# Two transformer layers on one core: where a layernorm's tiles are transposed, and what sums the attention heads

## The chip, the core and the metric

The kernel runs on one core of one Trainium2 chip. The metric is the device time of one launch in microseconds (us). Lower is better. The engines are named as in the profile: PE (TensorE, the matrix engine), DVE (VectorE), ACT (ScalarE), POOL (GpSimd) and SP (SyncE, which here only issues DMAs).

## The reference

Two layers over a sequence of 2048 tokens of 1024 features, with the same weights in both layers. Each layer is a sliding, dilated local attention and a dense block, each with a layernorm in front and a residual addition behind:

```python
x = x + attn(layernorm(x))     # wqkv: 1024 x 3072, wo: 1024 x 1024
x = x + dense(layernorm(x))    # w1: 1024 x 3584, gelu (tanh), w2: 3584 x 1024, b1, b2

# attn: 32 heads of 32 features; each token s sees 8 keys, at s, s-2, ..., s-14
logits[h, s, w] = sum_d q[h, s, d] * k[h, s - 2 * w, d] * scale      # masked where s - 2 * w < 0
p = softmax(logits, over w)
o[h, s, d] = sum_w p[h, s, w] * v[h, s - 2 * w, d]
```

## The kernel before

**Groups and stages.** A group is 512 tokens of one layer, so there are N = 8 groups, n = 0 to 7 (four for each layer). For each group PE runs four stages: qkv(n) (`gen_qkv`), WO(n) (`gen_wo`), FFN1(n) (`gen_ffn1`) and FFN2(n) (`gen_ffn2`). Their order on PE is written out by hand at the end of the kernel: qkv(0), qkv(1), the first 18 of 24 chunks of qkv(2), WO(0), the last 6 chunks of qkv(2) (they belong to V), FFN1(0), FFN2(0); then for n = 1 to 5: WO(n), qkv(n+2), FFN1(n), FFN2(n); then WO(6), WO(7), FFN1(6), FFN2(6), FFN1(7), FFN2(7). A chunk is one accumulator: 8 matmuls of 128x128 by 128x512 into one of six PSUM tiles `acc`, which ACT (qkv, FFN1) or DVE (WO, FFN2) empties.

**Order on the engines.** The stages are generators that yield after each chunk. `stage(gen, count, sides)` runs one and calls side functions after given chunks: `at(u, f, ...)` calls f after chunk u, `each(f, n, u0, du, c0, c1)` calls f(n, c) at regular chunks. PE's instructions keep the order in which the program issues them. ACT, DVE, POOL and SP are wrapped in `InOrder`, which can hold the same: `hold()` makes everything that DVE is given later come after what it was given before; between holds the scheduler orders DVE by itself. Every engine then works through its list in order, and an instruction that waits holds up all that stand behind it on that engine. `dep_order(a, b, why)` puts a behind b in the order of their engine without a wait.

**Layernorm and transposes.** Before qkv (`ln_a`) and after WO (inside `gen_wo`), `ln_tile` takes a tile of 128 tokens, computes its statistics (DVE), the inverse deviation `rstd` (POOL) and the normalized tile `xn` (DVE), and brings it into `xnT`, with the features on the partitions, as PE needs it. Usually that is one `dma_start_transpose` on SP's queue for each tile of 128x1024. In WO(0) only tiles 0 and 1 go this way; tiles 2 and 3 are put on the list `late`, and `transpose_late` transposes them on PE (`transpose_on_pe`: 8 matmuls with `ident` into an `acc`, then a copy by ACT), after chunk 4 of the last six chunks of qkv(2).

**Weights.** All weights stream through `wpool` (tile `wt`, five buffers of 1 MB) by DMAs on SP's queue, which also carries the transposes. FFN1 loads W1 in seven pieces, one for each four chunks (`j4`).

**Attention.** DVE multiplies q with eight shifted views of k, one product for each of eight feature slices c (`new_prod(n, c)`, tile `big`, three buffers), and adds the eight products in a tree. What is left holds, on 128 partitions, four feature parts of each of 32 heads, and these four must be summed. For groups 0 and 1 PE does it in `head_sum`: 8 matmuls of 128x32 by 128x512 with the 0/1 matrix `smat`, into the PSUM tile `L`. For groups 2 to 7 `gather(n)` issues four DMAs of 256 KB on POOL's queue which copy the product (SBUF to SBUF, `big<-big`) so that the four parts lie side by side, and `attend(n)` adds them by three DVE additions into `e`. `attend` then does the softmax (maximum and subtraction on DVE, Exp on ACT, sum, reciprocal and multiplication on DVE); `spread` copies the weights to all parts of a head through DRAM; `av(n, c)` multiplies them with eight shifted views of v and adds up the output `oT`. The sides of FFN1(n) hold attend(n+2) and most of av(n+1), those of qkv(n+2) the first av(n+1) and, by `gen_qkv`, the products of group n+2.

Of the kernel before, what the change touches and what calls it, by code (L numbers as in the profile page):

```python
# [17 lines left out]
def kernel(  # L18
# [188 lines left out]
    def transpose_on_pe(xn, out, pst=None, halves=1):  # L207
        if pst is None:
            pst = psum.tile([P, KD, P], BF16, name="acc", bufs=6)
        for k in range(KD):  # L210
            pe(nc.tensor.transpose(pst[:, k, :], xn[:, k * P:(k + 1) * P], ident[:]))
        n = KD // halves
        for h in range(halves):
            act.copy(out[:, h * n:(h + 1) * n, :], pst[:, h * n:(h + 1) * n, :])

    late = []

    def transpose_late():
        while late:
            transpose_on_pe(*late.pop(0))  # L220

    def ln_tile(t, tt, xnT, on_pe=False, ahead=False):
        mv, rstd = (mv_ahead[:, tt, :], rstd_ahead[:, tt, :]) if ahead else ln_stats(t)
        xn = ln_norm(t, mv, rstd)
        if on_pe:
            late.append((xn, xnT[:, tt, :, :]))
            return
        sp.dma_start_transpose(xnT[:, tt, :, :], xn[:].rearrange("s (k p) -> s k p", p=P))

    first_late = []  # L230

# [32 lines left out]
        assert len(a) == 2 and a[1][0] == 1 and a[1][1] == HALO + T  # L264
        return bass.AP(tensor=t_ap.tensor, offset=t_ap.offset, ap=[list(a[0]), [DIL, W], [1, T]])

    def win_by_tile(t_ap):
        a = t_ap.ap
        assert len(a) == 2 and a[1][0] == 1 and a[1][1] == HALO + T
        return bass.AP(tensor=t_ap.tensor, offset=t_ap.offset, ap=[list(a[0]), [P, NTT], [DIL, W], [1, P]])  # L270

    st = {n: {} for n in range(N)}
    xa = {}
    xb = {}
# [9 lines left out]
    def head_sum(n, last=True):  # L284

        if "L" not in st[n]:
            st[n]["L"] = psum.tile([P, W, P], F32, name="L", bufs=1)
            start = True
        else:
            start = False  # L290
        L = st[n]["L"]
        prod = st[n]["prods"].pop(0)
        for wh in range(2):
            for tb in range(NTT):
                mm(L[tb * H:(tb + 1) * H, wh * 4:(wh + 1) * 4, :], lhsT=smat[:],
                   rhs=prod[:, tb, wh * 4:(wh + 1) * 4, :], start=start,
                   stop=last, skip_group_check=True, tile_position=(0, tb * H))

    def new_prod(n, c):

        s = st[n]
        prod = bigp.tile([P, NTT, W, P], BF16, name="big")
        q = s["qT"][:, c, :].rearrange("p (b t) -> p b t", t=P)
        vec.tensor_tensor(out=prod[:], in0=q.unsqueeze(2).to_broadcast([P, NTT, W, P]), in1=win_by_tile(s["kT"][:, c, :]), op=ALU.mult)
        tree = s["prods"]
        tree.append(prod)
        if c % 2 == 1:
            for _ in range(1 if c % (NCH // s["parts"]) == 1 else 2):
                b = tree.pop()
                vec.tensor_tensor(out=tree[-1][:], in0=tree[-1][:], in1=b[:], op=ALU.add)  # L310
# [48 lines left out]
        if g + 1 < NG:  # L359
            act.copy(vhalo[:], vT[:, :, T:T + HALO])  # L360

    def gather(n):

        s = st[n]
        prod = s["prods"].pop(0)
        Lq = bigp.tile([P, HP, W, P], BF16, name="big")
        s["Lq"] = Lq
        for tb in range(NTT):
            pool.dma_start(Lq[tb * H:(tb + 1) * H, :, :, :], prod[:, tb, :, :])

    def attend(n):

        s = st[n]
        e = smp.tile([P, W, P], F32, name="e")
        if "Lq" in s:
            Lq = s.pop("Lq")
            vec.tensor_tensor(out=e[:], in0=Lq[:, 0, :, :], in1=Lq[:, 1, :, :], op=ALU.add)
            for j in range(2, HP):
                vec.tensor_tensor(out=e[:], in0=e[:], in1=Lq[:, j, :, :], op=ALU.add)
            L = e  # L380
        else:
            head_sum(n)
            L = s.pop("L")
        if n % NG == 0:
            vec.tensor_tensor(out=L[0:H, 0:W - 1, 0:HALO], in0=L[0:H, 0:W - 1, 0:HALO], in1=mask[:], op=ALU.add)
        mx = smp.tile([P, P], F32, name="mx")
        vec.tensor_reduce(out=mx[:], in_=L[:].rearrange("p w t -> p t w"), axis=AX.X, op=ALU.max)
        vec.tensor_tensor(out=e[:], in0=L[:], in1=mx[:].unsqueeze(1).to_broadcast([P, W, P]), op=ALU.subtract)
        act.activation(e[:], e[:], ACT.Exp, scale=SCALE)
        z = smp.tile([P, P], F32, name="z")  # L390
        vec.tensor_reduce(out=z[:], in_=e[:].rearrange("p w t -> p t w"), axis=AX.X, op=ALU.add)
        vec.reciprocal(z[:], z[:])
        a = smp.tile([P, W, P], BF16, name="a")
        vec.tensor_tensor(out=a[:], in0=e[:], in1=z[:].unsqueeze(1).to_broadcast([P, W, P]), op=ALU.mult)
        s["a"] = a
# [19 lines left out]
        vec.tensor_tensor(out=pv[:, 0:2, :], in0=pv[:, 0:2, :], in1=pv[:, 2:4, :], op=ALU.add)  # L415
        vec.tensor_tensor(out=s["oT"][:, c, :], in0=pv[:, 0, :], in1=pv[:, 1, :], op=ALU.add)

    def gen_wo(n, pe_from=NTT):
        g = n % NG
        oT = st[n]["oT"]  # L420
        wts = []
        for h in range(2):
            wt = wpool.tile([P, NCH // 2, D], BF16, name="wt")
            sp.dma_start(wt[:], wo_v[:, h * (NCH // 2):(h + 1) * (NCH // 2), :])
            wts.append(wt)
        xnT = new_xnT()
        xb[n] = xnT
        for tt in range(NTT):
            t = g * NTT + tt
            for dh in range(2):  # L430
                ps = acc_tile()
                for c in range(NCH):
                    mm(ps[:], lhsT=oT[:, c, tt * P:(tt + 1) * P], rhs=wts[c // 4][:, c % 4, dh * HALF:(dh + 1) * HALF],
                       start=(c == 0), stop=(c == NCH - 1))
                xs = x[t][:, dh * HALF:(dh + 1) * HALF]
                vec.tensor_tensor(out=xs, in0=ps[:], in1=xs, op=ALU.add)
                yield
            ln_tile(t, tt, xnT, tt >= pe_from)
        del st[n]

    def gen_ffn1(n):
        xnT = xb.pop(n)
        hT = hpool.tile([P, KF, T], BF16, name="hT")
        st[("h", n)] = hT
        for j4 in range(KF // 4):
            wt = wpool.tile([P, KD, 4 * P], BF16, name="wt")
            sp.dma_start(wt[:], w1_v[:, :, j4 * 4 * P:(j4 + 1) * 4 * P])
            for jj in range(4):
                j = j4 * 4 + jj
                ps = acc_tile()  # L450
                for k in range(KD):
                    mm(ps[:], lhsT=wt[:, k, jj * P:(jj + 1) * P], rhs=xnT[:, :, k, :], start=(k == 0), stop=(k == KD - 1))
                act.activation(hT[:, j, :], ps[:], ACT.Gelu_apprx_tanh, bias=b1T[:, j:j + 1])
                yield
# [63 lines left out]
    def stage(gen, count=None, sides=()):  # L518


        u = 0
        while count is None or u < count:
            if next(gen, gen) is gen:
                break
            for v, f in sides:
                if v == u:
                    f()
            u += 1
        for v, f in sides:
            if v >= u:  # L530
                f()
# [13 lines left out]
    with tc.tile_pool(name="early", bufs=1) as early:  # L545
        load_x(1)
        load_x(2)
        stage(gen_qkv(0, qk_next=early), sides=at(14, load_b2))
        q1 = gen_qkv(1, defer=True, qk_pool=early)
        stage(q1, sides=at(6, attend, 0) + at(6, spread, 0) + at(6, hold) + each(new_prod, 1, 8, 1, 0, 4) + each(av, 0, 12, 1))  # L550
        q2 = gen_qkv(2, defer=True)
        stage(q2, 18)
        stage(gen_wo(0, 2))
        stage(q2, sides=each(new_prod, 1, 0, 1, 4, 8) + at(4, transpose_late))
    hpool = ctx.enter_context(tc.tile_pool(name="hpool", bufs=1))
    stage(gen_ffn1(0), sides=at(4, attend, 1) + at(4, spread, 1) + at(4, hold) + each(new_prod, 2, 2, 1, 0, 4) + each(av, 1, 6, 2))
    stage(gen_ffn2(0), sides=at(0, ln_stats_ahead, 3) + at(15, hold) + each(new_prod, 2, 15, 1, 4, 8) + at(23, hold) + at(23, gather, 2) + at(23, ln_a, 3, None, True))
    for n in range(1, N - 2):
        stage(gen_wo(n), sides=at(0, spread, n + 1) if n > 1 else at(7, attend, 2))
        stage(gen_qkv(n + 2), sides=(at(0, spread, 2) if n == 1 else []) + each(av, n + 1, 0, 2, 0, 3))  # L560
        gather(n + 2)
        stage(gen_ffn1(n), sides=at(20 if n == 1 else 9, attend, n + 2) + each(av, n + 1, 8, 2, 3, 8))
        if n + 3 < N:
            stage(gen_ffn2(n), sides=at(2, ln_a, n + 3))
        else:
            stage(gen_ffn2(n), sides=at(0, spread, n + 2) + each(av, n + 2, 1, 4))
# [36 lines left out]
```

## Time and profile before

| | us |
|---|---|
| median of 8 runs | 1242.12 |
| lowest and highest run | 1241.39 and 1243.43 |
| the profiled execution's own time | 1243.43 |
| its span in the profile | 1241.7 |
| PE busy in the span | 1228.4 (99%) |
| DVE, ACT, POOL busy | 864.8, 306.1, 126.6 |

The mean clock that PE was granted is 0.999. In the timeline a line reads: start, duration, engine, line of the code, operation, output<-input, shapes, count; in brackets the idle time ahead of it and what ended it. Line L93 is the helper through which all of DVE's, ACT's, POOL's and SP's instructions go, and L118 the one for PE's matmuls, so that groups are told apart by their tiles. SPq is SP's sequencer, on which the DMAs are issued.

### The profile page before, as it was taken

Reading aid. Unit: us, or ns where it says so; the run is one execution under the profiler, and the core shown is the slowest. Engines: PE = TensorE matmul, PEld = TensorE weight load, DVE = VectorE, ACT = ScalarE, POOL = GpSimd, SP = SyncE. Lnnn points to the kernel's source line nnn. Section 1 sums busy time; section 2 is a strip of 40 time slices with the busy share of each in tenths; the row PEclk is TensorE's granted clock in tenths of the full one; section 3 lists DMA queues with packets and bytes.
Section 4 is the critical chain, followed back from the end, with each engine's and each line's share of the span. In section 5 each row is a group of like instructions: output and inputs, shape, how many; then the busy total and the mean of one; then the engine's idle time right before and its main releaser. Section 6 shows DMA issues by size and latency. Waiting matters only on the chain.

```text
span 1241.7 us, 13984 instructions
## 1 busy us (share of the span) xinstructions
PE 1228.4 (99%) x5793; PEld 632.6 (51%) x5793; DVE 864.8 (70%) x886; ACT 306.1 (25%) x477; POOL 126.6 (10%) x238
## 2 busy tenths in 40 slices
PE   9999999989999999999999999999999999999998
PEld 6666544446444564445644456444554444444444
DVE  7999899985994999457995469954599598012001
ACT  3333251013430133301342013410234101310310
POOL 4010210011031102200022000210000102000000
PEclk9999999999999999999999999999999999999999
DMA  9954564595577648655577465866646667546441
GB/s 300 285 178 149 167 203 155 168 200 178 180 185 223 167 157 218 195 169 153 170 209 208 165 172 167 206 196 192 195 159 167 195 199 193 168 156 195 148 138 53
DMA packets 217247, 226.10 MB, mean 182 GB/s; under 512 B 66450, under 2 KB 185376, under 8 KB 214112
## 3 DMA queue, kind: packets, MB, share of 16 engines
q1 hardware_dynamic: 212592, 208.16, 55.0%
q0 software_dynamic: 4592, 17.05, 6.1%
q8 instruction: 45, 0.74, 0.3%
q14 instruction: 18, 0.15, 0.0%
HBM read 197.40 MB, written 6.29 MB: 164 GB/s over the span
## 4 chain that ended last, share of the span: by engine, by line
PE 59%; DVE 6%; issue 0%; ACT 0%; POOL 0%; DVEq 0%
PE acc L118 59%; DVE big L93 4%; DVE stats L93 0%; DVE e L93 0%; POOL rstd L93 0%; DVE oT L93 0%; DVE mx L93 0%; ACT L93 0%; DVE xn L93 0%; ACT e L93 0%; ACT hT L93 0%; DVE x L93 0%; DVE mv L93 0%; DVEq L93 0%
## 5 line engine op out<-in xcount | busy, mean ns | idle before, releaser
L118 PE MATMUL acc<-xnT,wt 128*128 128x512 bf16 (+1 forms) x3376 | 722.2, 376 | 7.2 <-DMA xnT<-xn 4.9
L118 PEld LDWEIGHTS <-wt 128*128 128x128 bf16 x3376 | 399.2, 119 | 328.0 <-issue 10.3
L118 PE MATMUL acc<-wt,hT 128*128 128x512 bf16 (+1 forms) x1820 | 388.1, 376 | 0.0
L118 PEld LDWEIGHTS <-hT 128*128 128x128 bf16 x1820 | 178.1, 98 | 209.0
L93 DVE TENSOR_TENSOR big<-big 128x2048 bf16<-128x2048 bf16 (+2 forms) x184 | 246.4, 1361 | 2.6
L93 ACT ACTIVATE hT<-acc,b1T 128x512 bf16<-128x512 f32 x224 | 151.6, 690 | 310.3 <-PE acc L118 309.9
L93 DVE TENSOR_TENSOR big<-abc,vT 128x4096 bf16<-128x4096 bf16 x64 | 145.1, 2289 | 68.5 <-DMA abc<-a_d 67.9
L93 DVE TENSOR_TENSOR big<-qT,kT 128x4096 bf16<-128x4096 bf16 x64 | 143.8, 2287 | 26.7 <-ACT kT L93 26.1
L93 DVE TENSOR_TENSOR tmp<-acc,b2bc 128x512 f32<-128x512 f32 x56 | 38.7, 690 | 146.4 <-PE acc L118 143.4
L93 ACT CAST qT<-acc 128x512 bf16<-128x512 f32 x64 | 37.5, 587 | 320.8 <-PE acc L118 320.7
L118 PE MATMUL acc<-wt,oT 128*128 128x512 bf16 x448 | 97.8, 379 | 0.0
L93 DVE BATCH_NORM_STATS2 stats<-x 128x6 f32<-128x512 bf16 x128 | 83.0, 679 | 4.1 <-DMA x<-in_A_x_dram 3.7
L93 POOL TENSOR_TENSOR rstd<-mv,eps_t 128x1 f32<-128x1 f32 x60 | 27.5, 459 | 451.0 <-DVE mv L93 450.9
L118 PEld LDWEIGHTS <-oT 128*128 128x128 bf16 x448 | 43.8, 98 | 52.8
L93 DVE TENSOR_TENSOR x<-acc,big 128x512 bf16<-128x512 f32 (+1 forms) x9 | 5.7, 633 | 90.0 <-PE acc L118 90.0
L93 ACT CAST vT<-acc 128x512 bf16<-128x512 f32 x64 | 37.6, 587 | 83.6 <-PE acc L118 83.6
L93 ACT CAST kT<-acc 128x512 bf16<-128x512 f32 x64 | 37.6, 587 | 71.6 <-PE acc L118 71.6
L93 DVE TENSOR_TENSOR x<-acc,x 128x512 bf16<-128x512 f32 x64 | 42.9, 673 | 5.2 <-PE acc L118 5.0
L93 POOL DMA_DIRECT2D big<-big x24 | 13.7, 578 | 296.0 <-DVE big L93 237.1
L93 POOL TENSOR_TENSOR rstd<-rstd,mhalf 128x1 f32<-128x1 f32 x60 | 43.3, 722 | 4.7
L93 DVE TENSOR_SCALAR xn<-x,mv,rstd 128x1024 bf16<-128x1024 bf16 x52 | 28.1, 543 | 18.6 <-POOL rstd L93 17.0
L93 DVE TENSOR_TENSOR x<-tmp,x 128x512 bf16<-128x512 f32 x56 | 38.7, 691 | 1.3
(60 smaller groups left out, 251.9 us busy)
## 6 DMA issues: line engine op xcount, KB each, us to landing
wt<-in_B_w_dram SPq DMA_DIRECT2D x56, 1024.0 KB, 5.7
wt<-in_B_w_dram SPq DMA_DIRECT2D x64, 896.0 KB, 4.9
wt<-in_A_wqkv_dram SPq DMA_DIRECT2D x46, 1024.0 KB, 5.6
wt<-in_A_wo_dram SPq DMA_DIRECT2D x16, 1024.0 KB, 4.9
abc<-a_d POOLq DMA_DIRECT2D x32, 256.0 KB, 5.0
big<-big POOLq DMA_DIRECT2D x24, 256.0 KB, 7.5
x<-in_A_x_dram SPq DMA_DIRECT2D x16, 256.0 KB, 6.1
out_dram<-x SPq DMA_DIRECT2D x31, 128.0 KB, 2.7
```

Source lines behind the costliest of these rows:

```text
L93: inst = f(*args, **kwargs)
L118: return pe(nc.tensor.matmul(*args, **kwargs))
```

## The change

In WO(0) all four tiles are transposed by `dma_start_transpose`; `late`, `transpose_late` and the argument `pe_from` go. The second W1 load of FFN1(0) is put behind the last of these transposes in SP's order. One product of group 1 is issued ahead of WO(0) and three after it instead of four after it, with a `hold()` on each side of WO(0), so that DVE does only WO(0)'s additions and layernorm in between. `gather` and the three additions of `attend` go: for all groups `attend` calls `head_sum` on PE. The products change their layout from [tile of 128 tokens, w, token] to [w, token], and `head_sum` reads them accordingly.

```diff
-    late = []
-
-    def transpose_late():
-        while late:
-            transpose_on_pe(*late.pop(0))
-
-    def ln_tile(t, tt, xnT, on_pe=False, ahead=False):
+    last_transpose = [None]
+
+    def ln_tile(t, tt, xnT, ahead=False):
         mv, rstd = (mv_ahead[:, tt, :], rstd_ahead[:, tt, :]) if ahead else ln_stats(t)
         xn = ln_norm(t, mv, rstd)
-        if on_pe:
-            late.append((xn, xnT[:, tt, :, :]))
-            return
-        sp.dma_start_transpose(xnT[:, tt, :, :], xn[:].rearrange("s (k p) -> s k p", p=P))
+        last_transpose[0] = sp.dma_start_transpose(xnT[:, tt, :, :], xn[:].rearrange("s (k p) -> s k p", p=P))
...
                 mm(L[tb * H:(tb + 1) * H, wh * 4:(wh + 1) * 4, :], lhsT=smat[:],
-                   rhs=prod[:, tb, wh * 4:(wh + 1) * 4, :], start=start,
+                   rhs=prod[:, wh * 4:(wh + 1) * 4, tb * P:(tb + 1) * P], start=start,
                    stop=last, skip_group_check=True, tile_position=(0, tb * H))
...
-        prod = bigp.tile([P, NTT, W, P], BF16, name="big")
-        q = s["qT"][:, c, :].rearrange("p (b t) -> p b t", t=P)
-        vec.tensor_tensor(out=prod[:], in0=q.unsqueeze(2).to_broadcast([P, NTT, W, P]), in1=win_by_tile(s["kT"][:, c, :]), op=ALU.mult)
+        prod = bigp.tile([P, W, T], BF16, name="big")
+        vec.tensor_tensor(out=prod[:], in0=s["qT"][:, c, :].unsqueeze(1).to_broadcast([P, W, T]), in1=win(s["kT"][:, c, :]), op=ALU.mult)
...
-    def gather(n):
-
-        s = st[n]
-        prod = s["prods"].pop(0)
-        Lq = bigp.tile([P, HP, W, P], BF16, name="big")
-        s["Lq"] = Lq
-        for tb in range(NTT):
-            pool.dma_start(Lq[tb * H:(tb + 1) * H, :, :, :], prod[:, tb, :, :])
-
     def attend(n):
 
         s = st[n]
-        e = smp.tile([P, W, P], F32, name="e")
-        if "Lq" in s:
-            Lq = s.pop("Lq")
-            vec.tensor_tensor(out=e[:], in0=Lq[:, 0, :, :], in1=Lq[:, 1, :, :], op=ALU.add)
-            for j in range(2, HP):
-                vec.tensor_tensor(out=e[:], in0=e[:], in1=Lq[:, j, :, :], op=ALU.add)
-            L = e
-        else:
-            head_sum(n)
-            L = s.pop("L")
+        head_sum(n)
+        L = s.pop("L")
...
+        e = smp.tile([P, W, P], F32, name="e")
...
-            ln_tile(t, tt, xnT, tt >= pe_from)
+            ln_tile(t, tt, xnT)
...
-            sp.dma_start(wt[:], w1_v[:, :, j4 * 4 * P:(j4 + 1) * 4 * P])
+            load = sp.dma_start(wt[:], w1_v[:, :, j4 * 4 * P:(j4 + 1) * 4 * P])
+            if n == 0 and j4 == 1:
+                dep_order(load, last_transpose[0], "transposes first")
...
         stage(q2, 18)
-        stage(gen_wo(0, 2))
-        stage(q2, sides=each(new_prod, 1, 0, 1, 4, 8) + at(4, transpose_late))
+        new_prod(1, 4)
+        hold()
+        stage(gen_wo(0))
+        hold()
+        stage(q2, sides=each(new_prod, 1, 0, 1, 5, 8))
...
-    stage(gen_ffn2(0), sides=at(0, ln_stats_ahead, 3) + at(15, hold) + each(new_prod, 2, 15, 1, 4, 8) + at(23, hold) + at(23, gather, 2) + at(23, ln_a, 3, None, True))
+    stage(gen_ffn2(0), sides=at(0, ln_stats_ahead, 3) + at(15, hold) + each(new_prod, 2, 15, 1, 4, 8) + at(23, hold) + at(23, ln_a, 3, None, True))
...
-        gather(n + 2)
```

The calls of attend in the sides stand where they stood: attend(2) after chunk 7 of WO(1), attend(3) after chunk 20 of FFN1(1), attend(4) to attend(7) after chunk 9 of FFN1(2) to FFN1(5), with `head_sum` at those places in PE's order.

More of the change, by code (lines that the diff above doesn't have):

```diff
@@ L265, in win @@
         return bass.AP(tensor=t_ap.tensor, offset=t_ap.offset, ap=[list(a[0]), [DIL, W], [1, T]])
[L267 to L270, printed above, removed]
     st = {n: {} for n in range(N)}
@@ L416, in av, with gen_wo @@
         vec.tensor_tensor(out=s["oT"][:, c, :], in0=pv[:, 0, :], in1=pv[:, 1, :], op=ALU.add)
-    def gen_wo(n, pe_from=NTT):
+    def gen_wo(n):
         g = n % NG
```

## The prediction

> **What bounds the kernel now.** I read the busy table first, then TensorE's (PE's) waits, then the timeline around each wait, then one-microsecond windows.
>
> ```profile
> PE 1228.4 (99%) x5793; PEld 632.6 (51%) x5793; DVE 864.8 (70%) x886; ACT 306.1 (25%) x477; POOL 126.6 (10%) x238
> ```
>
> PE is busy 99% of 1241.7 us. Work taken off VectorE (DVE, 70%) or GpSimd (POOL) is worth nothing by itself; only PE's own work and PE's pauses count. The pauses, by what ended them:
>
> ```profile
> PE acc L118 <- DMA xnT<-xn: 4.9, 1, 4.9
> PE acc L118 <- ACT hT L93: 1.8, 1, 1.8
> PE acc L118 <- DVE big L93: 1.1, 1, 1.1
> PE acc L211 <- DVE xn L93: 1.0, 1, 1.0
> ```
>
> Columns are total, count, longest. The first: qkv(3) waits for its transposed input. The second: PE waits for ScalarE (ACT) in FFN1(2). The fourth stands at WO(0)'s PE transposes. The unit of PE's time is the matmul chunk: ACT's casts follow each other every 1.726 us, 8 matmuls of 0.2158.
>
> **Part 1: WO(0)'s tiles 2 and 3 leave PE.** Around the 16 PE transposes:
>
> ```profile
> 148.27 0.59 ACT L93 CAST vT<-acc 128x512 bf16<-128x512 f32 x1 [1.14 <-PE acc L118]
> 149.69 0.62 PE L211 MATMUL acc<-ident,xn 128*128 128x128 bf16 x8 [1.00 <-DVE xn L93]
> 152.08 0.59 ACT L93 CAST vT<-acc 128x512 bf16<-128x512 f32 x1 [0.72 <-PE acc L118]
> ```
>
> Two casts lie 3.81 us apart instead of 1.73: **-2.08 us** of PE (two groups of 8 transposes, 0.61 and 0.62, and the wait of 1.00). In their place two more DMA transposes stand on SyncE (SP), and the second W1 load behind the last. WO(0) ends on PE at 139.4; 48 matmuls of V follow (10.36), so FFN1(0) needs the tiles at 149.8. With DVE held to WO(0)'s adds and layernorm, the last xn is ready near 142.55; a DMA transpose lands in 2.7 (the shortest of the transposes' rows) to 4.4 us (their median): 145.3 to 147.0, margin 2.8 to 4.5. The moved W1 load is issued near 143.9 instead of 140.65 and lands 5.7 later (its row), at 149.6; FFN1(0) needs it at 149.8 + 4 x 1.726 = 156.7. Behind it on SP wait only later W1 loads. Cost of the move: nothing, hidden by the 10.36 us of V.
>
> [...]
>
> **The delayed DVE work.** new_prod(1,5) to (1,7) now come after WO(0)'s layernorm. Seven DVE operations (15.85 us by their rows: 2.25 for one product, 4.54 for two additions, 4.52 for two products, 4.54 for two additions) follow 142.55 and end at 158.4. PE demands head_sum(1) five chunks into FFN1(0), at 149.8 + 8.63 = 158.43. With a signal's passage **+0.2 us** (0 to 1).
>
> **Part 2: the gathers go.** The largest pause is in the timeline at qkv(3):
>
> ```profile
> 249.22 13.98 PE L118 MATMUL acc<-wt,oT 128*128 128x512 bf16 x64
> 254.18 13.98 SPq L93 DMA_TRANSPOSE xnT<-xn  x3
> 268.07 17.23 PE L118 MATMUL acc<-xnT,wt 128*128 128x512 bf16 x73 [4.87 <-DMA xnT<-xn]
> 271.30 0.59 ACT L93 CAST qT<-acc 128x512 bf16<-128x512 f32 x1 [29.34 <-PE acc L118]
> ...
> 407.51 13.98 PE L118 MATMUL acc<-wt,oT 128*128 128x512 bf16 x64
> 423.25 0.59 ACT L93 CAST qT<-acc 128x512 bf16<-128x512 f32 x1 [41.33 <-PE acc L118]
> ```
>
> From the start of WO(1) to the first qT cast of qkv(3) 22.08 us pass; the same stretch at WO(2), without a pause, takes 15.74. The pause costs **6.34 us**: 4.87 of wait, the rest PE at half clock after it. Why are the transposes late? gather(2) is issued by POOL at 246.9 to 249.4, just ahead of the transposes of ln_a(3) and WO(1). Windows (PE, PEld, DVE, ACT, POOL busy; PE clock; DMA share; GB/s):
>
> ```profile
> 137.00:138.00 1.00, 1.00 (x7) 0.46 (x5) 1.00 (x4) 0.00 (x0) 0.13 (x1) 1.00 0.68 151
> 253.00:254.00 1.00, 1.00 (x7) 0.42 (x5) 1.00 (x3) 0.00 (x0) 0.00 (x0) 1.00 1.49 138
> 256.00:257.00 1.00, 1.00 (x7) 0.41 (x6) 1.00 (x3) 0.00 (x0) 0.00 (x0) 1.00 1.02 100
> 265.00:266.00 1.00, 0.00 (x0) 0.00 (x0) 1.00 (x3) 0.00 (x0) 0.00 (x0) 1.00 1.03 401
> 268.00:269.00 1.00, 0.93 (x3) 0.47 (x4) 0.94 (x2) 0.00 (x0) 0.00 (x0) 0.50 1.27 285
> ```
>
> A lone transpose (137) moves 151 GB/s at a share of 0.68. At 253 to 257 a higher share moves only 100 to 138 GB/s, while weights alone (265) reach 401: the queues are clogged, and the slowest transpose lands after 15.6 us (median 4.4). Without the gather I expect ordinary landings. FFN2(0) now ends near 247.2; the fourth xn of ln_a(3) is issued about 6 us later and lands 3 to 5 us after that (256.2 to 258.5); PE needs it at 247.2 + 13.8 + one head sum, 261.7: margin 3 to 5. So **-6.34 us**. No later gather falls on transposes that PE waits for.
>
> **Part 3: the head sums come onto PE**, once each for groups 2 to 7. Groups 0 and 1 do it already:
>
> ```profile
> 64.59 0.62 PE L118 MATMUL L<-big,smat 128*32 128x512 bf16 x8
> 64.69 0.59 ACT L93 CAST qT<-acc 128x512 bf16<-128x512 f32 x1 [1.14 <-PE acc L118]
> 67.12 0.59 ACT L93 CAST qT<-acc 128x512 bf16<-128x512 f32 x1 [1.84 <-PE acc L118]
> ```
>
> The casts are 2.43 apart, 0.70 over 1.73; at group 1 (160.71 to 163.09) 0.65. 6 x 0.68 = **+4.08 us**, all on PE's path (bounds 3.9 and 4.2). The products' layout changes to suit; products of av, which read in that order already, take 2289 ns against 2287. [...]
>
> Each head sum must find its products added up. At group 3 they are ready at 330.8, PE asks at 339.3. For the others the products start when kT is cast; at qkv(5) the tree ends at 625.65, 9.0 us after FFN1(3) starts (616.65), and PE asks 17.3 us after it: margin 8.3.
>
> **Part 4: ACT's pause in FFN1(2).**
>
> ```profile
> 504.78 1.06 ACT L93 ACTIVATE e<-e 128x1024 f32<-128x1024 f32 x1
> 507.89 5.34 PE L118 MATMUL acc<-xnT,wt 128*128 128x512 bf16 x24 [1.80 <-ACT hT L93]
> ```
>
> The Exp, and a halo copy before it, stand in ACT's order ahead of gelus; they wait for DVE, six accumulators fill, PE stops 1.80 us. Three additions of 1.22 per group go, and the maximum reads PSUM in 1.22 instead of 1.91 (group 0's row). In the changed order DVE runs, after the tree (9.0 us into FFN1): two av (8.55), two multiplies (4.41), maximum (1.2), an addition (1.14), the subtraction (1.2): 25.5. Exp follows at 25.6; it must start by 28.65 for gelu 12 to free its accumulator before chunk 18. Margin 3.1 us (3.9 in FFN1(2)); the halo copy has 3.7. So **-1.80 us**.
>
> Off the path: DVE loses 18 x 1.22 + 6 x 0.69 = 26 us, POOL 24 issues (13.7 us), the DMA queues 6.3 MB; PE was waiting for none of it elsewhere.
>
> **Sum**: -2.08 + 0.2 - 6.34 + 4.08 - 1.80 = -5.94. The profiled execution took 1243.43 (span 1241.7 and 1.73 around it), so 1237.5 on its basis; the median of the eight runs is 1242.12, so **1236.2**.
>
> **Rivals.** *The gather is not to blame*: the transposes queue behind weight loads, the 6.34 stays, and the sum is -2.08 + 0.2 + 4.08 - 1.80 = +0.4: 1242.5. For it: WO(1)'s weights are in flight at the same time. Against: transposes beside weight loads elsewhere (366 to 378, 568 to 581, 1026 to 1056) cost PE nothing. If half stays: 1239.4.
>
> *Exp blocks ACT in every FFN1(2) to (5)* (the slower side): it stands in front of gelu 12, and PE stops once Exp starts later than 28.65 us into the stage. If DVE is 5.3 us later than worked, each of four stages loses 2.2, 8.8 in all: 1245.0. For it: before has one such stop. Against: 3.1 us of margin, and DVE has idle stretches of 7.06 us ahead of the products to absorb layernorm work:
>
> ```profile
> 591.59 6.70 DVE L93 TENSOR_TENSOR big<-qT,kT 128x4096 bf16<-128x4096 bf16 x3 [7.06 <-ACT kT L93]
> ```
>
> *The 1.80 merely moves* to another FFN1, or head_sum(1) waits 1 us: 1237 to 1238.0. *The DMA transposes of WO(0) land late*: from the issue at 142.6 they have 7.2 us; a landing as slow as the worst row, 15.6, would cost 8.4 and end at 1244.6, but that row has a gather beside it, and none is near here.
>
> **How the numbers follow.** Forecast (with the moved 1.80) 0.70; all of the 6.34 staying 0.10, half 0.06; Exp blocking or late landings 0.14. About 0.2% (2.5 us) is what a measurement of this kernel can tell: faster 0.76, same 0.10, slower 0.14. The range runs from 1234.6 (cheapest head sums, no new wait, and the runs' own spread) to 1241.0, which holds the forecast, the moved stall and half of the 6.34; the likeliest case's own range is 1235.2 to 1238.0.
>
> **What would show it.** PE's waits should hold no line "DMA xnT<-xn" near 4.9 and no "ACT hT" near 1.8; L should show 64 PE matmuls with smat, not 16, with about 0.68 between casts each; from WO(1)'s start to the first qT cast 16.4 (15.74 and the head sum that now stands there) and not 22.1 us. A wait for xnT at qkv(3) proves the first rival; a wait for ACT hT in FFN1(2) to (5) the second; a wait for DVE big over 1 us at 158 the late products.

## The result and the profile after

The changed kernel takes 1237.64 us (median of 11 runs, 1237.49 to 1238.11). In the same series the kernel before takes 1242.04 (median of 32 runs, 1237.76 to 1244.67). The ratio is 0.997 (95% interval 0.996 to 0.9981): 4.4 us faster, against a forecast of 5.9. The profiled execution took 1237.65, with a span of 1235.9.

The busy table and PE's waits of the changed kernel:

```profile
PE 1229.2 (99%) x5825; PEld 631.8 (51%) x5825; DVE 840.5 (68%) x868; ACT 304.2 (25%) x475; POOL 93.0 (8%) x214
```

```profile
PE L L118 <- DVE big L93: 1.1, 1, 1.1
PE acc L118 <- DVE big L93: 1.1, 1, 1.1
PE acc L211 <- POOL rstd L93: 1.0, 1, 1.0
PE acc L118 <- ACT xnT L93: 0.6, 1, 0.6
```

The waits for xnT (4.9), for ACT hT (1.8) and, at WO(0)'s transposes, for DVE xn (1.0) are gone. One line is new: `L <- DVE big`, 1.1 us, which is head_sum(1). The others belong to the first 10 us. The timeline of WO(1), beside that of before in the prediction:

```profile
247.97 13.98 PE L118 MATMUL acc<-wt,oT 128*128 128x512 bf16 x64
255.57 0.55 DVE L93 TENSOR_SCALAR xn<-x,mv_ahead,rstd_ahead 128x1024 bf16<-128x1024 bf16 x1 [2.05 <-DMA xnT<-xn]
261.88 0.62 PE L118 MATMUL L<-big,smat 128*32 128x512 bf16 x8
264.41 0.59 ACT L93 CAST qT<-acc 128x512 bf16<-128x512 f32 x1 [22.62 <-PE acc L118]
```

From the start of WO(1) to the first qT cast it is 16.44 us, head sum included (forecast 16.4; 22.08 before). The second line carries a warning: DVE's fourth xn still waits 2.05 us for the transposes, because xn has three buffers.

Since PE hardly ever rests, the starts of WO(n) and FFN2(n) in PE's timeline cut the span into stages that can be compared between kernels to about 0.02 us. All that follows rests on this table, in us, one profiled execution each. Column A runs from WO(0) to FFN2(0), B from WO(1) to FFN2(1), C from WO(2) to FFN2(2), D is the same for n = 3 to 5 (equal in all three to 0.01). FFN2(n) itself takes 48.35 everywhere.

| kernel | median | span | to WO(0) | A | B | C | D |
|---|---|---|---|---|---|---|---|
| before | 1242.04 | 1241.7 | 125.63 | 75.25 | 109.94 | 105.56 | 103.60 |
| changed | 1237.64 | 1235.9 | 125.31 | 74.31 | 104.95 | 104.25 | 104.25 |
| before, profiled again | 1241.95 | 1240.0 | 125.36 | 75.41 | 108.32 | 105.54 | 103.60 |
| before, group 2 summed on PE | 1236.36 | 1235.1 | 126.23 | 75.24 | 104.30 | 104.07 | 103.60 |
| before, WO(0)'s part alone | 1244.63 | 1242.6 | 125.31 | 74.30 | 111.96 | 105.87 | 103.60 |
| before, all sums on PE | 1238.83 | 1237.0 | 125.27 | 75.24 | 104.95 | 104.26 | 104.26 |
| changed, with idle copies in SBUF | 1246.53 | 1245.5 | 125.27 | 74.33 | 114.54 | 104.25 | 104.25 |
| changed, with idle loads from DRAM | 1239.40 | 1237.1 | 125.35 | 74.30 | 106.10 | 104.26 | 104.25 |
| changed, sums twice | 1241.32 | 1239.4 | 125.78 | 74.74 | 105.82 | 104.69 | 104.69 |
| changed, attend(1) later | 1236.68 | 1235.3 | 125.35 | 73.18 | 105.43 | 104.26 | 104.26 |
| changed, group 4 gathered | 1237.06 | 1235.3 | 125.29 | 74.33 | 104.97 | 103.60 | 104.26 |
| changed, group 3 gathered | 1238.32 | 1236.7 | 125.57 | 74.30 | 104.30 | 105.37 | 104.25 |
| 3, 5, 6, 7 gathered, attend(1) later | 1235.31 | 1234.1 | 125.92 | 73.35 | 104.30 | 105.39 | 103.60 |
| 4 to 7 gathered, attend(1) later | 1234.08 | 1232.7 | 125.70 | 73.27 | 104.96 | 103.60 | 103.60 |

From before to changed, in the two profiled executions: -0.32 to WO(0) (the start, which differs by up to 1.0 between these runs), -0.94 in A, -4.99 in B, -1.31 in C, +0.65 three times in D: -5.6 of the spans' -5.8; what is left lies behind WO(6).

### The profile page after: what moved, and what is told of

Read it like the earlier page. It is cut to its first block, busy times and chain, and to the rows that moved or that the text cites. A ratio compares the mean times of both kernels' runs of the same rounds, so it can differ in the third digit from the quotient of the medians.

```text
span 1235.9 us, 14011 instructions
## 1 busy us (share of the span) xinstructions
PE 1229.2 (99%) x5825; PEld 631.8 (51%) x5825; DVE 840.5 (68%) x868; ACT 304.2 (25%) x475; POOL 93.0 (8%) x214
## 4 chain that ended last, share of the span: by engine, by line
PE 97%; DVE 2%; POOL 0%; issue 0%; DMA 0%; ACT 0%
PE acc L118 96%; DVE big L93 1%; DVE stats L93 1%; PE L L118 0%; DVE x L93 0%; POOL rstd L93 0%; DMA x<-in_A_x_dram 0%; DVE xn L93 0%; DVE mv L93 0%; PE acc L211 0%; PE L L211 0%; ACT xnT L93 0%
## 5 line engine op out<-in xcount | busy, mean ns | idle before, releaser
L93 DVE TENSOR_TENSOR big<-big 128x1024 bf16<-128x1024 bf16 (+2 forms) x184 | 244.4, 1361 | 1.8
L93 POOL TENSOR_TENSOR rstd<-mv,eps_t 128x1 f32<-128x1 f32 x60 | 14.5, 242 | 500.8 <-DVE mv L93 500.8
L93 POOL DMA_DIRECT2D a_d<-a x32 | 19.5, 631 | 416.6 <-DVE a L93 416.6
L93 DVE TENSOR_SCALAR xn<-x,mv,rstd 128x1024 bf16<-128x1024 bf16 x52 | 28.3, 544 | 27.7 <-POOL rstd L93 27.4
L93 POOL TENSOR_TENSOR rstd<-rstd,mhalf 128x1 f32<-128x1 f32 x60 | 33.9, 565 | 4.7
```

Source lines behind the costliest of these rows:

```text
L93: inst = f(*args, **kwargs)
```

## The experiments

**Does the pause of qkv(3) scatter?** The runs of before lie within 7 us, those of the changed kernel within 0.6. The kernel before was profiled again, unchanged.

> The kernel before, unchanged, profiled once more, because its runs scatter over 7 us (1237.8 to 1244.7) where those of the changed kernel lie within 0.6. Theory: the scatter is the wait of qkv(3) for xnT, which the gather of group 2 makes now short, now long; in this profile the line xnT<-xn of PE's waits differs from 4.9 us by about as much as the span differs from 1241.7 (less half as much again for the half clock after it), and the wait for ACT hT stays at 1.8. Rival: the scatter lies elsewhere (start, weights), and the wait for xnT stays at 4.9 whatever the span.

```profile
PE acc L118 <- DVE x L93: 3.2, 1, 3.2
PE acc L118 <- ACT hT L93: 1.8, 1, 1.8
```

The ratio is 0.9999 (0.9986 to 1.0013). In this execution the pause stands at the same place, 3.25 us long and with another name on it (DVE x, where it was DMA xnT), while ACT hT is 1.8 again. Stage B fell by 1.62, the span by 1.7; the other stages agree to 0.2 but for the start. So the pause of qkv(3) is what differed between these two executions. That it makes the whole scatter is not shown run by run, but it fits two things. The granted clock that is on record for each of these twelve runs is 1.0 for the four that took up to 1240.65 us, and 0.997 to 0.999 for the eight from 1241.66 up, so PE was at a lower clock for part of the longer runs, as it is behind the pause of the first profile (0.50 from 268 to 270), though this does not tell where. And the runs below are steady once gather(2) is gone.

**Group 2 alone summed on PE.**

```diff
-    ... + at(23, hold) + at(23, gather, 2) + at(23, ln_a, 3, None, True))
+    ... + at(23, hold) + at(23, ln_a, 3, None, True))
```

> The kernel before with the head sum of group 2 alone on PE, the gathers of groups 3 to 7 kept. Theory: gather(2) slows the transposes of qkv(3); without it -6.34 + 0.68, span near 1236.0, time near 1237.8, runs within about 1 us of each other; the wait for ACT hT of 1.8 stays or shrinks a little. First rival (weight loads slow the transposes): the wait for xnT stays near 4.9 and the time is near 1242.7 and scatters as before.

```profile
PE acc L118 <- DVE big L93: 1.1, 1, 1.1
PE acc L211 <- DVE xn L93: 1.0, 1, 1.0
PE acc L118 <- ACT xnT L93: 0.6, 1, 0.6
PE acc L211 <- POOL rstd L93: 0.5, 1, 0.5
PE acc L118 <- ACT hT L93: 0.3, 1, 0.3
```

1236.36 (1235.92 to 1236.82), ratio 0.996 (0.9946 to 0.9973). No wait at qkv(3), B is 104.30: one head sum over 103.60. The first rival (weight loads slow the transposes) is out, since all weights still load there. This one line of the change gives more than all of the change together.

**The copies put back, idle.** To the changed kernel four DMAs were added that copy the same products into a free buffer; nothing reads it.

```diff
+    def copy_parts(n):
+        prod = st[n]["prods"][0]
+        Lq = bigp.tile([P, W, T], BF16, name="big")
+        for tb in range(NTT):
+            pool.dma_start(Lq[tb * H:(tb + 1) * H, :, :], prod[:, 2 * tb:2 * tb + 2, :].rearrange("p a t -> p (a t)"))
...
+    ... + at(23, hold) + at(23, copy_parts, 2) + at(23, ln_a, 3, None, True))
```

> The changed kernel with four DMAs of 256 KB on GpSimd's queue added where gather(2) stood, from the same products into a free buffer; nothing reads what they copy. Theory: the collision comes back without anything else of before: a wait for xnT at qkv(3) of 0 to 7 us, times from 1237.6 up to 1244, median 1 to 6 us above 1237.64, scattered. Rival (it was the place of the additions on VectorE or the weights, not the copies): 1237.6 and steady, no wait for xnT.

```profile
246.72 2.48 POOL L93 DMA_DIRECT2D big<-big  x4 [56.24 <-DVE xn L93]
262.55 0.55 DVE L93 TENSOR_SCALAR xn<-x,mv_ahead,rstd_ahead 128x1024 bf16<-128x1024 bf16 x1 [9.06 <-DMA xnT<-xn]
264.94 6.56 PE L118 MATMUL acc<-wt,oT 128*128 128x512 bf16 x16 [6.47 <-DVE tmp L93]
```

1246.53 (1245.73 to 1247.5), ratio 1.0043 (1.003 to 1.0057): the copies alone cost the changed kernel 8.9 us, more than the 6.3 that I had counted and beyond the expected 1237.6 to 1244, and steadily, where scatter was expected. The three lines are the chain: POOL issues the copies; the transposes are slow; DVE's fourth xn has no free buffer and waits 9.06 us; behind it in DVE's order stand most of the operations that empty FFN2(0)'s and WO(1)'s accumulators; PE stops in WO(1), for 6.47.

**WO(0)'s part alone**, on the kernel before (its edits are those of the diff above, with `gather` and the additions left in).

> The kernel before with WO(0)'s part of the change alone (all four tiles by DMA, the W1 load behind them, the two holds), all gathers kept. Theory: -2.08 for the transposes and +1.07 for the wait of head_sum(1) that the changed kernel shows, so 1.0 us less than before in a like run, with the scatter of before (median 1240 to 1242, since the wait for xnT stays); PE's waits hold xnT (0 to 7) and DVE big 1.1 at head_sum(1), none for WO(0)'s transposes. Rival (these transposes land late): a wait for xnT near 149.8 of several us.

```profile
262.45 0.55 DVE L93 TENSOR_SCALAR xn<-x,mv_ahead,rstd_ahead 128x1024 bf16<-128x1024 bf16 x1 [8.95 <-DMA xnT<-xn]
264.84 5.46 PE L118 MATMUL acc<-wt,oT 128*128 128x512 bf16 x16 [6.36 <-DVE tmp L93]
```

When the copies and the transposes of ln_a(3) were issued, first in the kernel before, then in this run:

```profile
246.78 6.68 SPq L93 DMA_TRANSPOSE xnT<-xn  x3
246.94 2.48 POOL L93 DMA_DIRECT2D big<-big  x4 [58.94 <-DVE xn L93]
```

```profile
246.74 2.47 POOL L93 DMA_DIRECT2D big<-big  x4 [56.24 <-DVE xn L93]
248.57 15.68 SPq L93 DMA_TRANSPOSE xnT<-xn  x4
```

1244.63, ratio 1.0025 (1.0014 to 1.0036): slower, against an expected gain of 1.0. WO(0)'s own stage did what was worked out (A is 74.30, as in the changed kernel). The loss is more than 100 us later, in B: 111.96. The chain is the same as with the idle copies. In this order of the program all four xn of ln_a(3) go out after a weight load on SP, 1.8 us behind the first copy, where in the kernel before they are issued 0.16 us ahead of it. The fourth xn stands ahead of most of WO(1)'s emptying on DVE, and with gather(2) it waits 8.95 us (3.02 in the kernel before). That this order of issue makes the copies cost more is likely, but no run changes it alone. The two parts of the change are therefore not additive: WO(0)'s part is a loss while gather(2) is there, and a gain without it.

**All sums on PE, WO(0) as before** (the diff above without WO(0)'s edits).

> The kernel before with all head sums on PE, no gather, and WO(0) left as it was (tiles 2 and 3 transposed on PE). By the changed kernel's trace WO(0)'s part saved 2.08 and gave back 1.1 to head_sum(1): this should be 0.9 to 1.0 us slower than the changed kernel, 1238.6, with no wait for xnT and none for ACT hT. If WO(0)'s part carries more of the gain: 1239.7 or more; if none: 1237.6.

1238.83 (1238.67 to 1239.36), ratio 0.9981 (0.9968 to 0.9993): 1.2 us above the changed kernel, 0.93 of it in A, the rest below what one can place. WO(0)'s part is worth about 1 us in the changed kernel.

**Head sums done twice.**

```diff
-        for wh in range(2):
+        for wh in list(range(2)) * 2:
```

> The changed kernel with each of the eight head sums done twice (the same 8 matmuls again into the same L), to price one. If what a head sum costs is all in its matmuls (0.65 us each), 8 x 0.65 = +5.2: 1242.8. If part of it is the change from full to 32-column matmuls and back, the second pass is cheaper; 8 matmuls of which four run beside each other would be 0.43, +3.5: 1241.1. The demands stand where they stood, so no new wait is expected.

1241.32, ratio to before 0.9995 (0.9984 to 1.0006), 3.7 above the changed kernel. In the stages an extra pass costs 0.43 to 0.44 (C and D: 104.69 - 104.25), not 0.65. So of the 0.65 us of one head sum 0.43 are its 8 matmuls, a quarter of the 8 x 0.2158 us of a chunk. The other 0.22, by subtraction, comes once for each head sum and not with a second pass; whether it is the change to 32 columns and back, as the expectation allowed for, no run shows.

**attend(1) one chunk later.**

```diff
-    stage(gen_ffn1(0), sides=at(4, attend, 1) + at(4, spread, 1) + at(4, hold) + ...
+    stage(gen_ffn1(0), sides=at(5, attend, 1) + at(5, spread, 1) + at(5, hold) + ...
```

> The changed kernel with attend(1), its spread and its hold one chunk later in FFN1(0) (after chunk 5 instead of 4). Theory: the wait of 1.07 us of head_sum(1) for its products goes, since PE asks 1.73 us later: 1237.64 - 1.1 = 1236.5. Rival: the products follow PE's demand or the later softmax holds up FFN1(0)'s gelus, and the time stays at 1237.6 or rises.

1236.68 (1236.61 to 1237.02), ratio 0.9963 (0.9951 to 0.9976), 0.96 below the changed kernel. A lost 1.13, the wait; B rose by 0.48, with a new wait of 0.3 for `DVE tmp` in WO(1):

```profile
248.69 1.46 DVE L93 TENSOR_SCALAR xn<-x,mv_ahead,rstd_ahead 128x1024 bf16<-128x1024 bf16 x3
250.80 10.52 PE L118 MATMUL acc<-wt,oT 128*128 128x512 bf16 x47 [0.31 <-DVE tmp L93]
```

DVE comes to the first three xn of ln_a(3) 2.66 us later than in the changed kernel (246.03), and the first emptying behind them, which ends at 250.74, is now late for WO(1). The fourth xn finds its buffer free here, without a wait.

**Which gather makes ACT's pause?** Part 4 of the prediction put the pause of FFN1(2) down to group 4's additions. First group 4 alone was gathered again in the changed kernel, then group 3 alone:

```diff
+    GATHERED = {4}      # then {3}; new_prod, gather and attend of before for these groups
```

> The changed kernel with group 4 gathered again (old product layout, four copies, three additions on VectorE), all other groups on PE. Theory (part 4 of the prediction): a head sum less is -0.65, and the pause for ACT hT in FFN1(2) comes back, as the additions put Exp later in ScalarE's order: 0.5 (as with group 2 alone on PE) to 2.0 (as before): 1237.5 to 1239.0, with a line ACT hT in PE's waits. If the pause has nothing to do with group 4's additions: no such line, 1237.0.

> The changed kernel with group 3 alone gathered again. Gathering group 4 alone brought no pause in FFN1(2), and the version with groups 3, 5, 6 and 7 had one of 1.0; so the theory is now that the pause comes from group 3: its additions stand late in FFN1(1), its softmax ends some 20 us later, its av work is pushed into group 4's products, and Exp(4) comes too late. Then -0.65 for the head sum and +0.5 to +2.0 for the pause, with a line ACT hT in PE's waits: 1237.5 to 1239.0. Rival (it needs the gathers of groups 3 and 4, or 5, together): no such line, 1237.0.

With group 4, 1237.06 (1237.01 to 1237.5), ratio 0.9967 (0.9954 to 0.9979), C is 103.60 and PE's waits hold no line ACT hT. With group 3, 1238.32, ratio 0.9977 (0.9965 to 0.999), C is 105.37, and PE's waits and ACT's timeline in FFN1(2) show (the last line is of the kernel before):

```profile
PE acc L119 <- ACT hT L94: 1.0, 1, 1.0
```

```profile
466.31 0.28 ACT L94 COPY kT<-khalo 128x112 bf16<-128x112 bf16 x1 [5.85 <-DVE big L94]
485.87 1.06 ACT L94 ACTIVATE e<-e 128x1024 f32<-128x1024 f32 x1 [6.19 <-DVE e L94]
```

```profile
502.59 0.29 ACT L93 COPY vT<-vhalo 128x112 bf16<-128x112 bf16 x1 [7.86 <-DVE big L93]
```

So gathering group 3 brings such a pause by itself, and gathering group 4 does not. Group 3's three additions are issued late in FFN1(1), and on DVE they stand behind av work; the last operation of its softmax on DVE is, in the kernel before, the changed one, the changed one with group 3 gathered, and the kernel before with group 2 alone on PE:

```profile
387.49 1.22 DVE L93 TENSOR_TENSOR a<-e,z 128x1024 bf16<-128x1024 f32 x1
```

```profile
366.31 1.22 DVE L93 TENSOR_TENSOR a<-e,z 128x1024 bf16<-128x1024 f32 x1
```

```profile
377.51 1.21 DVE L94 TENSOR_TENSOR a<-e,z 128x1024 bf16<-128x1024 f32 x1
```

```profile
375.97 1.21 DVE L93 TENSOR_TENSOR a<-e,z 128x1024 bf16<-128x1024 f32 x1
```

What follows on DVE, av(3) and group 4's products, moves back, ACT's copies and its Exp wait for DVE, and the accumulators fill. What counts is how late DVE is against PE. Counted from the start of FFN2(1) on PE, the line starts after 13.4 us in the changed kernel (no pause), 21.9 with group 2 alone on PE (0.3), 25.0 with group 3 alone gathered (1.0), 28.3 in the kernel before (1.8) and 30.1 with WO(0)'s part alone (2.1): the later, the longer the pause. So the pause of 1.8 in the kernel before is not group 3's alone: with gather(2) away and group 3 still gathered, 0.3 of it is left. Which instruction of ACT waits differs as well: in the kernel before it is the halo copy for vT, with Exp right behind it, and with group 3 alone gathered it is Exp.

**Two versions with gathers where they do no harm.** Both have attend(1) one chunk later; the first gathers groups 3, 5, 6, 7 (run before group 3's part was known), the second 4 to 7.

> The changed kernel with groups 3, 5, 6 and 7 gathered again (no transposes that PE waits for fall beside these copies), groups 0, 1, 2 and 4 summed on PE, and attend(1) one chunk later. Theory: -4 x 0.65 - 1.1 = -3.7: 1233.9, steady, below both kernels. Rival (the gathers hurt wherever they stand): a wait for xnT or DVE in qkv(4) to qkv(7), 1236 or more.

> The changed kernel with groups 4 to 7 gathered again, groups 0 to 3 summed on PE, attend(1) one chunk later. If group 3's gather alone makes the pause of FFN1(2): no wait for ACT hT, 4 x 0.65 less than with attend(1) later alone (1236.68): 1234.1. If the pause needs only some gather near: 1235 to 1236.

The first: 1235.31, ratio 0.9952 (0.994 to 0.9965), 1.4 above what was expected; C is 105.39 with the pause of 1.0 for ACT hT. The second: 1234.08 (1233.9 to 1234.41), ratio 0.9944 (0.9923 to 0.9964). It meets its sum, and is 3.6 us below the changed kernel and 8.0 below the one before. All that PE waits for:

```profile
PE acc L119 <- DVE big L94: 1.1, 1, 1.1
PE acc L119 <- ACT xnT L94: 0.6, 1, 0.6
PE acc L212 <- POOL rstd L94: 0.3, 1, 0.3
PE L L212 <- ACT xnT L94: 0.2, 1, 0.2
```

All four lie in the first 15 us. (In these versions the helpers' lines are numbered one higher.)

**Must it be a copy within SBUF?** The idle copies once more, reading weights from DRAM.

```diff
+            pool.dma_start(Lq[tb * H:(tb + 1) * H, :], B_w2[tb * P:(tb + 1) * P, :].rearrange("(p c) f -> p (c f)", c=4))
```

> The changed kernel with four DMAs of 256 KB on GpSimd's queue where gather(2) stood, as in the run with four copies from the products, but reading weights from DRAM instead of the products in SBUF; nothing reads what they bring. If any DMA of this size on that queue slows the transposes: a wait of several us in WO(1) or qkv(3), 1244 to 1247.5. If it must be a copy from SBUF to SBUF: 1237.6 to 1239.

```profile
244.36 2.31 POOL L93 DMA_DIRECT2D big<-in_B_w_dram  x4 [53.84 <-DVE big L93]
257.11 0.55 DVE L93 TENSOR_SCALAR xn<-x,mv_ahead,rstd_ahead 128x1024 bf16<-128x1024 bf16 x1 [3.57 <-DMA xnT<-xn]
```

1239.40 (1238.8 to 1239.81), ratio 0.9983 (0.9971 to 0.9994): +1.8, between the two expectations. DVE's fourth xn waits 3.57 (2.05 without, 9.06 with the SBUF copies). It is no clean answer: without products to wait for, these loads were issued 2.4 us earlier (244.36 against 246.72), 4.2 us ahead of the first transpose instead of 1.8. Whether the source or the moment makes the difference stays open.

## Why the prediction was right, and where it was not

**WO(0)'s transposes (-2.08): right.** V's casts follow each other at 147.96 and 149.68, 1.72 apart, and FFN1(0) did not wait for xnT or its weights. With attend(1) later, where head_sum(1) does not wait, A is 2.07 below that of the kernel before. The last three of these transposes landed in 2.9 us (median; the slowest of WO(0)'s four in 4.2), within the 2.7 to 4.4 of the prediction, and since that lay beside other work it cost PE nothing.

**head_sum(1) (+0.2): too small, by 0.9.**

```profile
154.68 4.62 DVE L93 TENSOR_TENSOR big<-big 128x4096 bf16<-128x4096 bf16 x2
159.35 0.61 PE L118 MATMUL L<-big,smat 128*32 128x512 bf16 x8 [1.07 <-DVE big L93]
```

The seven operations took 16.0 us (worked: 15.85). What was mis-sized is their start: the last xn ended at 143.39, not 142.55, since its statistics were complete at 141.9 and `rstd` took 0.93 more. Products and demand had been worked out to within 0.05 us of each other, so that any lateness went straight to PE; the bounds of 0 to 1 should have been 0 to 2, with the middle taken. The 0.2 for a signal's passage was my estimate and no run shows it: DVE's last addition ended at 159.30, and PE began 0.05 later, at 159.35.

**gather(2) (-6.34): right in cause, too large in the median.** Group 2 alone on PE removes the pause, and idle copies alone bring one back, there in WO(1), through the late fourth xn; so the cause is shown. But 6.34 is the pause of one execution out of a scattering kernel, and one from the upper part of it: 1243.43 against a median of 1242.04. The step that failed is the last line of the sum. It took the 1.3 us between profile and median off the changed kernel as well, as if that were a constant of the measurement. By the second profile, where B alone fell by 1.62, and by the clocks of the runs, it was part of the pause, and left with it: on the profile's own basis the forecast was 1237.5, and 1237.64 was measured. The span would have been 1235.8 by this sum and is 1235.9. That it comes so close is partly luck: the 0.9 too much at head_sum(1) was made up by things that the sum did not hold or had a little too dear, 0.3 less to WO(0), 0.2 less behind WO(6), 0.2 less in C and 0.1 less in D.

The place of the margin was also wrong. I took it to be where the transposes land before qkv(3) (3 to 5 us; by the prediction's own numbers the late end of the landing is 258.2, not 258.5, which changes nothing). The tight place is one step earlier, and the prediction gave it no wait: the fourth xn on DVE, waiting 2.05 us for a buffer, with WO(1)'s accumulators behind it. It came out at 256.1. One at 257.7 already cost PE a wait of 1.0 (with the loads from DRAM).

**Head sums (+4.08): right.** By the stages, 2 x 0.675 in B and 4 x 0.65 in C and D: 3.95. Of the head sums that moved, none waited. For cheaper ones, which the range took in at its lower end (1234.6), no run shows a price: only a second pass over the same products took less, 0.43 to 0.44.

**ACT's pause (-1.80): right in size (C without its head sum fell by 1.96), wrong in cause.** It is gone, and Exp(4) starts at 482.64, which is 26.1 us into FFN1(2) (28 chunks and a head sum, 48.33 + 0.65 us, before its FFN2 at 505.52); worked out were 25.6. But group 4's three additions, to which the prediction gave the credit, are harmless: gathered alone in the changed kernel they leave C at 103.60. It was DVE's lateness behind group 3's softmax, to which the gathers of groups 3 and 2 both add. I followed the wait back to the nearest DVE operations and stopped there, without asking why DVE came to them late.

**The rivals.** The gather not to blame: out, by group 2 alone on PE. Exp blocking ACT: it did not happen in the changed kernel, yet it is real, and came at the point that was named: with group 3 gathered, Exp starts 29.7 us into FFN1(2) (485.87, the stage starting 48.33 + 0.65 + 1.12 before 506.24), past the 28.65 set, and PE stops for 1.0. Late DMA transposes in WO(0): out. The 1.80 did not move to another FFN1, since D holds one head sum and nothing more. But the other half of that rival came true: head_sum(1) waits 1.07 us, and the 1237.64 lies in the 1237 to 1238.0 that went with it; the sign named for late products, a wait for DVE big over 1 us at 158, is in PE's waits.

## What to carry to other kernels

A pause in one profiled execution of a kernel whose runs scatter has no single size (4.87 and 3.25 us in two executions here): look at the spread first, and do not carry the distance between profile and median over to a kernel that no longer has the pause. When a buffer is waited for, ask which instructions stand behind the waiting one on its engine; with the idle copies, transposes that were slow cost time only through an xn that waited (9.06 us) and the accumulators behind it (6.47 on PE). And undo a change of several parts part by part: the six head sums that moved to PE cost about 0.65 us each, and only those of groups 2 and 3 brought more than that.

## What the runs showed of the hardware

**The pauses of 3.25 to 6.47 us cost 1.3 to 1.5 times their length, and in the three whose windows are given here PE's clock was at half for 3.42, 6.82 and 10.24 us.** Windows of the version with idle SBUF copies (length of the window; PE, PEld, DVE, ACT, POOL busy; PE clock; DMA share; GB/s):

```profile
260.00:261.00 1.00, 0.00 (x0) 0.00 (x0) 0.00 (x0) 0.00 (x0) 0.00 (x0) 0.85 1.84 99
265.00:266.00 1.00, 1.00 (x3) 0.34 (x3) 1.00 (x3) 0.00 (x0) 0.75 (x2) 0.50 0.37 80
270.00:271.00 1.00, 1.00 (x4) 0.42 (x3) 0.93 (x3) 0.00 (x0) 0.82 (x2) 0.53 0.00 0
271.00:272.00 1.00, 1.00 (x12) 0.15 (x10) 1.00 (x2) 0.00 (x0) 0.00 (x0) 1.00 0.82 57
```

The clock reads 1.00 from 259 to 260, 0.50 in each window from 261 to 270 and 1.00 from 271 to 273, so a mean of 0.85 at 260 to 261 puts the fall from full to half at 260.70, and 0.53 at 270 to 271 the rise at 270.94. In between are 10.24 us, and PE worked 6.0 of them at half speed: half of that and the wait of 6.47 make 9.5 of the 9.59 us that stage B lost. The same reckoning gives 6.82 us at half clock with WO(0)'s part alone (0.89 at 261 to 262, 0.70 at 268 to 269) and 3.42 in the kernel before (0.65 at 267 to 268, 0.64 at 270 to 271): the longest is three times and the middle one twice the shortest, to 0.02 us. In the second profile of the kernel before the wait of 3.25 cost 4.72 (108.32 - 103.60), 1.47 more than its length, as much as the wait of 4.87 in the first (6.34). From the start of the wait to the fall of the clock 2.2 (idle copies), 3.3 (WO(0)'s part) and 4.1 us (before) went by. The stretches tell why waits of nearly the same length (6.36 and 6.47) cost 8.36 (111.96 - 103.60) and 9.59 (114.54 - 104.95). In the waits of 1.07 us at head_sum(1) (changed kernel), 0.98 in WO(1) (loads from DRAM) and 1.80 in FFN1(2) (kernel before) the clock stayed at 1.00, and they cost 0.06, 0.17 and 0.16 us more than their length.

**Copies on GpSimd's queue made transposes on SyncE's land later.** Four copies of 256 KB, 1 MB in all, held DVE's fourth xn for 9.06 us where it waits 2.05 without them, and the slowest transpose of that run landed after 13.9 us (in the changed kernel 7.9 for the slowest from 245 to 275, 11.8 in the whole run). How the two share the DMA engines was not isolated. In the page of the kernel before GpSimd's queue has 17.05 MB in 4592 packets (3.7 KB each), the hardware queue 208.16 MB in 212592 (1.0 KB); from 230 to 270, where GpSimd's queue carries the copies alone, it has 1.05 MB in 320 packets (3.3 KB). What of this makes the transposes late, no run shows.
